# Attention with a gated dense branch on one core: keys packed 128 rows to a projection and spread through DRAM, values two groups at a time, and a higher threshold for giving up units

## The chip, the cores and the metric

The kernel runs on one core of one Trainium2 chip. Its time is the time in microseconds (us) of one execution on the device; the median of several runs is compared. Lower is better. The core has five engines that work side by side, each through its own list of instructions in order: PE (TensorE, matmuls), ACT (ScalarE), DVE (VectorE), POOL (GpSimd) and SP (SyncE, which here only issues DMAs). Engines wait for each other by semaphores.

## What is computed

Two branches work on the same x, and a gate per token mixes them.

```python
# x: 2048 x 640, bf16; 32 heads of 20; dense width 1536
g = sigmoid((x * gate_w).sum(-1, keepdims=True))
qkv = (x @ wqkv).reshape(1, 2048, 3, 32, 20)          # -> q, k, v per head
p = softmax(einsum("bhqd,bhkd->bhqk", q, k) * 20 ** -0.5)
a = einsum("bhqk,bhkd->bhqd", p, v).reshape(1, 2048, 640) @ wo
h = x @ w1 + b1
b = (h * tanh(softplus(h))) @ w2
out = g * a + (1 - g) * b
```

There are 32 × 2048 × 2048 exponentials. They are the largest part of the work.

## The kernel before

**Units, slots and steps.** The 32 heads are eight groups of four. A group's keys and queries lie in KT and QT, each head on its own 32 partitions, of which 20 hold data. A *unit* is the 128 × 512 scores of one head, one block of 128 keys and one block of 512 queries. A *slot* holds three units in three banks of PS. A *step* handles one slot: PE writes its scores (L947), ACT takes one exponential over all three units into ETS (L969), and later PE multiplies by the values, four heads side by side, into one bank (L1072, an attention pass). There are 2048 units, so 683 steps. The first 341 steps take the query blocks 0 and 1 group by group, the others the blocks 2 and 3.

**Units given up by ACT.** In some steps the third unit isn't ACT's: DVE computes its exponential with a chain of six instructions (L986, L1001, three of L1003, L1004). ACT's exponential of that step is then two units wide (128 × 1024 instead of 128 × 1536). `choose` decides it.

**The order is planned when the kernel is built.** A planner (`Plan`, `attention`) goes through the steps in Python, holds an estimate of each engine's time, and writes the list of instructions of each engine. All work other than scores, exponentials and passes is a *task*: a few matmuls into one spare bank of PS and an instruction, mostly of DVE, that empties it. A task has a due step. A forced one is put in at its due step at the latest; before that, tasks go into the gaps of PE. From the tasks' due steps the planner works out how far PE is behind (`behind`), and gives a unit up before the step `slot_of(0, 1, 0)` freely and after it only where, among others, `behind < CATCH_UP` (L1364). Where the planner sees that PE would stream too little, it adds filler matmuls: it repeats scores, or spins on keys (L1315).

**Projections.** A task of `kq_task` (L516) makes the keys or the queries of one group and one block of 512 tokens: POOL first copies the group's 80 weight columns into PADK or PADQ with each head moved to its 32 columns (L500), then five 512-column matmuls (L522) yield 128 rows, of which 80 hold data, and DVE copies them into KT or QT (L533). A task of `v_task` (L592) makes one group's values for 512 tokens with 20 matmuls of 80 columns (L597), and DVE puts them into V_all (L605). Group 0's first block is made at the start (`first_keys`). The tasks for w1, the dense branch and the output projections follow, the last of them in the second half.

**Normalisation.** When a group's passes are done, DVE copies the sums to OUNG (L1150). SP fetches the row of sums into RR (L1153), DVE takes the reciprocal (L1157), SP writes it to SUMS in DRAM (L1158) and reads it back spread over partitions into BCT (L1160), and DVE multiplies (L1118) into OTN or QT. These three DMAs and all loads of weights are in SP's one list, in the planner's order.

Of the kernel before, what the change touches and what calls it, by code (L numbers as in the profile page):

```python
# [9 lines left out]
BF16 = mybir.dt.bfloat16  # L10
# [6 lines left out]
P = 128  # L17
S = 2048
D = 640
# [45 lines left out]
AHEAD = 14  # L65
BEHIND = 7.0
PATIENCE = 10.0
CATCH_UP = 2.0
BUSY = 0.6
CROWD = 1.4  # L70
MARGIN = 0.5
# [7 lines left out]
LAG = 8  # L79
WINDOW = 3.41  # L80
CALM = 4
THIN = 0.09
CUTS = ((0, 256), (256, 256))

# [119 lines left out]
def bass_gated_mix__softmax_full_mha__dense_activation_mish__prompt_kernel(  # L204
# [116 lines left out]
    def attention(pl, fast):  # L321
# [37 lines left out]
        def real(g):  # L359
            return min(g, NG - 1)  # L360
# [14 lines left out]
        def later(step, fn):  # L375
            at.setdefault(step, []).append(fn)
# [50 lines left out]

        k_done, q_done, v_done = {}, {}, {}
        k_more = []
        x_read = {c: [] for c in range(NC)}  # L430
        wkv_read, wq_read = [], []
        xt_load = [None] * NC
# [10 lines left out]
        if fast:  # L443
# [70 lines left out]
            gw_col = pl.add("pool", lambda e: e.tensor_copy(WV[:, :, D], GW[:, :]), [g_load])  # L514

            def kq_task(k, g, c, due, forced=True):  # L516
                b = g % 2
                dst = (QT, KT)[k]
                pads = (PADQ, PADK)[k]

                def mm(f):
                    return lambda e, bank: e.matmul(  # L522
                        PS[:, bank, :], pads[:, b, f, :], xt(c)[:, f, :], start=(f == 0), stop=(f == NFT - 1))
# [12 lines left out]

                return Task([mm(f) for f in range(NFT)], PASS, finish, due,
                            lambda: [*xt_load[c], pad(k, g)], forced)

            turned = []  # L540

# [50 lines left out]
            def v_task(g, c, due):  # L592
# [8 lines left out]
                def finish(bank, last):  # L601
# [12 lines left out]

                return Task([mm(t, f) for t in range(4) for f in range(NFT)], 0.036, finish, due,
                            lambda: [*xt_load[c], w_load["wv0" if g == 0 else "wv"]] + [gw_col] * (n > HD), True)

            def sigmoid(got):
                ex = pl.add("act", lambda e: e.activation(GATE[:, :], GT1[:, :], AF.Exp, scale=-1.0), [got], cost=0.2)
# [438 lines left out]
        def pv(some):  # L1058
# [4 lines left out]
            for r in range(CW // w):  # L1063
                for n, ((_, _, kt, j), src, deps) in enumerate(some):
# [7 lines left out]
                    lasts[n] = pl.add("pe", lambda e, tile=tile, h=real(g) * HG + j, j=j, src=src[:, cols], of_q=of_q, count=count: e.matmul(  # L1072
# [33 lines left out]
        def group_done(c, g, step, last):  # L1106
# [61 lines left out]
        if fast:  # L1168
# [20 lines left out]
            tasks.extend(sq_task(n, 24 + 16 * n) for n in range(8))  # L1189
            tasks.extend(h_task(hc, k, 150 + int(12.5 * (6 * hc + k))) for hc in range(2) for k in range(6))  # L1190
            tasks.sort(key=lambda t: t.due)
            later(60, lambda: (load_w1(0), load_w1(1)))
            rest = []

            def mixed(a, b):
# [137 lines left out]
        for step in range(NSLOT + 40):  # L1333
# [13 lines left out]
            if fast and step == 6:  # L1347
# [207 lines left out]
```

## Time and profile before

| what | us |
|---|---|
| median of 3 runs | 910.29 |
| the runs | 906.25, 912.21, 910.29 |
| the profiled execution | 907.12 |
| its span, first to last instruction | 905.3 |
| ACT busy | 887.6 |
| DVE busy | 813.8 |
| PE busy | 763.3 |
| exponentials (L969) busy, 683 of them | 870.3 |

The profile shows one execution. A group of instructions has a line, an engine, an operation, the tiles that it writes and reads, a count, its busy time and the mean length of one in ns; behind it stands how long the engine was idle just before, and for whom. Lengths of neighbours on one engine can overlap, so the distance between two starts is the better price of one instruction. "Granted clock" is the share of its full clock that PE was given.

### The profile page before, as it was taken

What the parts mean: (1) busy time and instruction counts of PE and PEld (TensorE: products, weight loads), DVE (VectorE), ACT (ScalarE), POOL (GpSimd) and SP (SyncE); (2) the same over time, 40 slices, a digit from 0 to 9 for tenths busy, and PEclk for the clock granted to TensorE, in tenths of its full rate; (3) what the DMA queues carried; (4) which work ended last, traced back from release to release, by engine and by line L of the source; (5) the groups of instructions that cost most, each with busy time, mean ns of one, the idle gap of its engine ahead of it and who ended that gap; (6) DMA issues with size and microseconds to landing.
All of it is one profiled execution on the core that took longest, in us unless ns stands there. A gap on an engine that the chain in (4) does not pass through costs nothing.

```text
span 905.3 us, 15709 instructions
## 1 busy us (share of the span) xinstructions
PE 763.3 (84%) x6516; PEld 263.9 (29%) x6516; DVE 813.8 (90%) x1473; ACT 887.6 (98%) x714; POOL 15.0 (2%) x28
## 2 busy tenths in 40 slices
PE   8878888888888888888888888888888888888886
PEld 3222222232323223222332232232232323333322
DVE  5995859989699999999999999999999999987695
ACT  6999999999999999999999999999999999999996
POOL 2000000000000000000000000000000000000000
PEclk9999999999999999999999999999999999999998
DMA  9002000010101100014111130211121201200001
GB/s 224 4 13 42 13 14 13 6 37 14 42 28 37 35 28 13 13 39 116 47 43 53 46 80 22 57 38 31 51 68 40 71 13 56 57 20 24 13 14 33
DMA packets 63518, 36.44 MB, mean 40 GB/s; under 512 B 19992, under 2 KB 59424, under 8 KB 63392
## 3 DMA queue, kind: packets, MB, share of 16 engines
q1 hardware_dynamic: 61072, 34.88, 14.1%
q8 instruction: 53, 0.87, 0.4%
q10 hardware_dynamic: 2256, 0.47, 0.3%
q0 software_dynamic: 112, 0.01, 0.2%
q14 instruction: 25, 0.20, 0.1%
HBM read 30.25 MB, written 2.89 MB: 37 GB/s over the span
## 4 chain that ended last, share of the span: by engine, by line
ACT 96%; PE 3%; DMA 0%; issue 0%; DVE 0%; SPq 0%; ACTq 0%
ACT ETS L969 93%; ACT REG L761 2%; PE PS L947 1%; PE PS L822 1%; ACT W2R L761 1%; PE PS L1072 1%; DMA OTN<-in_A_x_dram 0%; PE PS L798 0%; PE PS L571 0%; DVE HB L828 0%; PE PS L1315 0%; PE PS L562 0%; PE PS L550 0%; SPq L452 0%; ACT KT L546 0%
## 5 line engine op out<-in xcount | busy, mean ns | idle before, releaser
L969 ACT ACTIVATE ETS<-PS 128x1536 bf16<-128x1536 f32 (+1 forms) x683 | 870.3, 1592 | 3.5 <-PE PS L947 3.3
L947 PE MATMUL PS<-QT,KT 32*128 32x512 bf16 (+1 forms) x2222 | 280.9, 381 | 129.1 <-ACT ETS L969 115.9
L1072 PE MATMUL PS<-ETS,V_all 128*21 128x512 bf16 (+1 forms) x1973 | 210.2, 382 | 0.1
L947 PEld LDWEIGHTS PS<-QT,KT 32*128 32x128 bf16 x2222 | 69.7, 91 | 345.1 <-ACT ETS L969 324.0
L1003 DVE SCALAR_TENSOR_TENSOR EM<-EM 128x512 f32<-128x512 f32 (+1 forms) x201 | 138.3, 688 | 0.4 <-DVE QT L533 0.2
L1003 DVE SCALAR_TENSOR_TENSOR ER<-ER 128x512 f32<-128x512 f32 (+1 forms) x198 | 135.4, 684 | 0.1
L1072 PEld LDWEIGHTS PS<-ETS,V_all 128*21 128x21 bf16 x1973 | 48.9, 89 | 101.9 <-issue 97.4
L798 PE MATMUL PS<-W2R,HB 128*128 128x320 bf16 x384 | 72.1, 305 | 1.0 <-DVE XB L805 0.3
L729 PE MATMUL PS<-XB,REG 128*128 128x256 bf16 x360 | 54.0, 275 | 1.5 <-DVE HB L739 0.9
L522 PE MATMUL PS<-XB,REG 128*128 128x512 bf16 x155 | 47.8, 385 | 0.0
L522 PE MATMUL PS<-XB,WOQ 128*128 128x512 bf16 x155 | 46.6, 384 | 0.0
L781 DVE RECIPROCAL T<-T 128x256 f32<-128x256 f32 x24 | 41.9, 1747 | 0.0
L798 PEld LDWEIGHTS PS<-W2R,HB 128*128 128x128 bf16 x384 | 29.5, 98 | 36.4 <-issue 22.1
L986 DVE TENSOR_SCALAR XE<-PS 128x512 f32<-128x512 f32 x52 | 35.7, 687 | 3.7 <-PE PS L947 3.3
L533 DVE CAST KT<-PS 128x512 bf16<-128x512 f32 x31 | 21.4, 690 | 19.5 <-PE PS L522 19.3
L729 PEld LDWEIGHTS PS<-XB,REG 128*128 128x128 bf16 x360 | 29.2, 97 | 26.0 <-issue 23.0
L597 PE MATMUL PS<-REG,XB 128*128 128x80 bf16 (+1 forms) x640 | 33.7, 201 | 1.8 <-DVE KT L533 0.6
L739 DVE TENSOR_TENSOR HB<-PS,B1F 128x512 bf16<-128x512 f32 x48 | 33.0, 687 | 1.1 <-PE PS L729 0.9
L986 DVE TENSOR_SCALAR REG<-PS 128x512 f32<-128x512 f32 x45 | 30.8, 685 | 0.7 <-PE PS L947 0.7
L597 PEld LDWEIGHTS PS<-REG,XB 128*128 128x128 bf16 x640 | 25.8, 98 | 17.4 <-issue 9.4
L1150 DVE COPY OUNG<-PS 128x512 f32<-128x512 f32 x31 | 21.3, 687 | 9.4 <-PE PS L1072 9.2
L986 DVE TENSOR_SCALAR W2R<-PS 128x512 f32<-128x512 f32 x36 | 24.8, 688 | 3.6 <-PE PS L947 3.5
(115 smaller groups left out, 690.6 us busy)
## 6 DMA issues: line engine op xcount, KB each, us to landing
REG<-in_B_w_dram SPq DMA_DIRECT2D x36, 320.0 KB, 3.2
BCT<-SUMS SPq DMA_DIRECT2D x31, 256.0 KB
W2R<-in_B_w_dram SPq DMA_DIRECT2D x12, 320.0 KB, 3.2
W2R<-in_B_w_dram SPq DMA_DIRECT2D x1, 1920.0 KB, 8.1
out_dram<-OUTT SPq DMA_DIRECT2D x24, 80.0 KB, 1.6
REG<-in_A_wqkv_dram SPq DMA_DIRECT2D x2, 700.0 KB, 8.5
WOQ<-in_A_wo_dram SPq DMA_DIRECT2D x4, 200.0 KB
WOQ<-in_A_wqkv_dram SPq DMA_DIRECT2D x1, 700.0 KB, 8.1
```

Of the source, the lines that this page charges most:

```text
L522: return lambda e, bank: e.matmul(PS[:, bank, :], pads[:, b, f, :], xt(c)[:, f, :], start=(f == 0), stop=(f == NFT - 1))
L597: return lambda e, bank: e.matmul(PS[:, bank, t * n:(t + 1) * n], xt(c)[:, f, t * P:(t + 1) * P], WV[:, f, g * HD:g * HD + n], start=(f == ...
L729: return lambda e, bank: e.matmul(PS[:, bank, i * HW:(i + 1) * HW], w1b(n1)[:, f, i * P:(i + 1) * P], xt(c)[:, f, cols], start=(f == 0), s ...
L739: ev = dve(lambda e: e.tensor_tensor(hb, PS[:, bank, :].rearrange("p (i t) -> p i t", i=2), bias, ALU.add), [last, *b1f, *sq_read.values() ...
L761: ex = pl.add("act", lambda e: e.activation(U, h, AF.Tanh, scale=0.5), [ev, u_free[0]], cost=0.95)
L781: piece(RECIP, lambda e: e.reciprocal(T1[:, :], T1[:, :]))
L798: return lambda e, bank: e.matmul(PS[:, bank, 0:HALF], HB[:, hc % 2, f, t * P:(t + 1) * P], W2[:, f, half * HALF:(half + 1) * HALF], start ...
L947: op = pl.add("pe", lambda e, i=i, g=real(g), tile=tile, j=j, cols=cols, c=c, of_q=of_q: e.matmul(scores(s)[:, i, cols], KT[32 * j:32 * j ...
L969: e_op[s] = pl.add("act", lambda e: e.activation(ETS[:, s % NETS, 0:n, :], scores(s)[:, 0:n, :], AF.Exp, scale=SCALE), [s_op[s], pv_slot.g ...
L986: ev_op[s] = dve(lambda e: e.tensor_scalar(y, scores(s)[:, 2, :], SCALE * ULPS, BIAS, ALU.mult, ALU.add), [s_op[s], ei_free[b], *(wkv_read ...
L1003: piece(WIDE, lambda e, v=m if i else f, i=i: e.scalar_tensor_tensor(m, v, STEPS[i], v, ALU.add, ALU.mult))
L1072: lasts[n] = pl.add("pe", lambda e, tile=tile, h=real(g) * HG + j, j=j, src=src[:, cols], of_q=of_q, count=count: e.matmul(PS[32 * j:32 * ...
```

## The change

Keys of the groups 1 to 7 are no longer padded before the projection. `k_task` projects 128 plain rows at once (weight columns 80 to 591 in four tasks per token block), and `k_end_task` the last 48 rows for two token blocks side by side. DVE copies the result to one of four stages in OTN (rows that the groups 6 and 7 will use later), SP writes the stage to KS in DRAM (`shelve`), and three steps after the last piece of a group's keys was written SP reads them back into KT (`fetch`), 32 rows for each head at a stride of 20. The 12 rows that a head has too many are those of the next head; they meet rows of QT that are zero. The tasks are due ten steps before their keys are needed (`PACKED`), where `kq_task` had three. Values of the groups 2 to 7 are projected for two groups at once, three tiles of 128 tokens in a task (`v_pair_task`). `CATCH_UP` goes from 2 to 3. `SQ`, `SQ_STEP`, `H_AT` and `H_STEP` name numbers that are the same as before.

```diff
-CATCH_UP = 2.0
+CATCH_UP = 3.0
...
+PACKED = 10
...
+    KS = nc.dram_tensor("KS", [NC, D + DH, CW], BF16, kind="Internal")
...
             def kq_task(k, g, c, due, forced=True):
-                b = g % 2
+                b = 0 if k else g % 2
...
-                    if c == NC - 1 and g + 2 < NG:
+                    if not k and c == NC - 1 and g + 2 < NG:
                         pad(k, g + 2)
...
+            stages = [OTN[:, a, b, :] for b in (6, 7) for a in range(2)]
+            stage_free, k_written, k_reads = {}, {}, {}
+            k_need = {1: (0,), 2: (0, 1), 3: (1,), 4: (1, 2), 5: (2, 3), 6: (3,), 7: (3, "end")}
+            count = [0]
+            none = ZEROS.ap()[:, 0:CW]
+            k_blank = [pl.add("sp", lambda e, c=c: e.dma_start(
+                KS.ap()[c, D:D + 12, :], none.to_broadcast([12, CW])), [zeros], "kz", cost=0.5) for c in range(NC)]
+
+            def shelve(name, c, rows, src, ev, n, i=0):
+
+                k_written[(name, c)] = pl.add(
+                    "sp", lambda e: e.dma_start(KS.ap()[c, rows, :], src), [ev], f"kw{n}{i}", cost=0.5)
+                k_moved.append(k_written[(name, c)])
+                stage_free.setdefault(n, []).append(k_moved[-1])
+                for g, names in k_need.items():
+                    if (g, c) not in k_done and name in names and all((m, c) in k_written for m in names):
+                        k_done[(g, c)] = None
+                        later(now["step"] + 3, lambda g=g, c=c, names=names: fetch(g, c, names))
+
+            def fetch(g, c, names):
+
+                at = KS.ap()[c, g * HD:(g + 1) * HD, :].rearrange("(j r) t -> j r t", r=DH)
+                at = bass.AP(tensor=at.tensor, offset=at.offset, ap=[list(at.ap[0]), [at.ap[1][0], 32], list(at.ap[2])])
+                slot = f"kr{c}{g % 2}"
+                k_done[(g, c)] = k_reads[slot] = pl.add(
+                    "sp", lambda e: e.dma_start(KT[:, g, c * CW:(c + 1) * CW], at),
+                    [*(k_written[(m, c)] for m in names), *k_blank, k_reads.get(slot)], slot, cost=0.5)
+
+            def k_task(i, c, due):
+
+                base = HD + P * i
+
+                def mm(f):
+                    return lambda e, bank: e.matmul(
+                        PS[:, bank, :], WK[:, f, base:base + P], xt(c)[:, f, :], start=(f == 0), stop=(f == NFT - 1))
+
+                def finish(bank, last):
+                    x_read[c].append(last)
+                    wkv_read.append(last)
+                    n = count[0] % 4
+                    count[0] += 1
+                    ev = dve(lambda e: e.tensor_copy(stages[n], PS[:, bank, :]), [last, *stage_free.pop(n, ())], WIDE)
+                    shelve(i, c, slice(base, base + P), stages[n], ev, n)
+                    return ev
+
+                return Task([mm(f) for f in range(NFT)], PASS, finish, due, lambda: [*xt_load[c], w_load["wk"]], True)
+
+            def k_end_task(c, due):
+
+                base, m = HD + 4 * P, D - HD - 4 * P
+
+                def mm(f, i):
+                    return lambda e, bank: e.matmul(
+                        PS[64 * i:64 * i + m, bank, :], WK[:, f, base:D], xt(c + i)[:, f, :],
+                        start=(f == 0), stop=(f == NFT - 1), tile_position=(0, 64 * i))
...
-                    v_done[(g, c)] = ev
+                    v_done.update({(g, c * 4 + t): ev for t in range(4)})
...
+            def v_pair_task(g, tiles, due):
+
+                n = 2 * HD + (g == NG - 2)
+                cs = sorted({t // 4 for t in tiles})
+
+                def mm(i, t, f):
+                    return lambda e, bank: e.matmul(
+                        PS[:, bank, i * n:(i + 1) * n], xt(t // 4)[:, f, t % 4 * P:(t % 4 + 1) * P],
+                        WV[:, f, g * HD:g * HD + n], start=(f == 0), stop=(f == NFT - 1))
...
-                        deps = [*deps, v_done[(real(g), tile // 4)]]
+                        deps = [*deps, v_done[(real(g), tile)]]
...
-                    return [low_last[0]] if c >= 2 else [zeros, *turned]
+                    return [low_last[0]] if c >= 2 else [zeros, *turned, *(k_moved if g >= 6 else ())]
...
-                        tasks.append(kq_task(1, g, c, due - 3))
-                        tasks.append(v_task(g, c, due - 1))
-                        last_kv = tasks[-1]
+                        if g == 0:
+                            tasks.append(kq_task(1, g, c, due - 3))
+                        if g < 2:
+                            tasks.append(v_task(g, c, due - 1))
...
+            for i, g in enumerate((1, 2, 4, 5)):
+                tasks.extend(k_task(i, c, slot_of(0, g, 4 * c) - PACKED) for c in range(NC))
+            tasks.extend(k_end_task(c, slot_of(0, NG - 2, 4 * c) - PACKED) for c in (0, 2))
+            for g in range(2, NG, 2):
+                for t in range(0, NKT, 3):
+                    tasks.append(v_pair_task(g, list(range(t, min(t + 3, NKT))), slot_of(0, g, t) - 1))
+            last_kv = tasks[-1]
```

More of the change, by code (lines that the diff above doesn't have):

```diff
@@ L81 @@
 CALM = 4
+PACKED = 10
+SQ = 24
+SQ_STEP = 16
+H_AT = 150
+H_STEP = 12.5
 THIN = 0.09
@@ L429, in attention @@
         k_more = []
+        k_moved = []
         x_read = {c: [] for c in range(NC)}
@@ L516, in kq_task @@
             def kq_task(k, g, c, due, forced=True):
-                b = g % 2
+                b = 0 if k else g % 2
                 dst = (QT, KT)[k]
@@ new lines, in k_end_task, with finish @@
+            def k_end_task(c, due):
[4 more added lines that the diff above has]
+                        start=(f == 0), stop=(f == NFT - 1), tile_position=(0, 64 * i))
+                def finish(bank, last):
+                    wkv_read.append(last)
+                    n = count[0] % 4
+                    count[0] += 1
+                    for i in range(2):
+                        x_read[c + i].append(last)
+                    ev = dve(lambda e: e.tensor_copy(stages[n], PS[:, bank, :]), [last, *stage_free.pop(n, ())], WIDE)
+                    for i in range(2):
+                        shelve("end", c + i, slice(base, D), stages[n][64 * i:64 * i + m, :], ev, n, i)
+                    return ev
+                return Task([mm(f, i) for f in range(NFT) for i in range(2)], PASS / 2, finish, due,
+                            lambda: [*xt_load[c], *xt_load[c + 1], w_load["wk"]], True)
@@ L616, in v_task, with finish @@
                             lambda: [*xt_load[c], w_load["wv0" if g == 0 else "wv"]] + [gw_col] * (n > HD), True)
+            def v_pair_task(g, tiles, due):
[5 more added lines that the diff above has]
+                        WV[:, f, g * HD:g * HD + n], start=(f == 0), stop=(f == NFT - 1))
+                def finish(bank, last):
+                    for c in cs:
+                        x_read[c].append(last)
+                    wkv_read.append(last)
+                    m = len(tiles)
+                    got = PS[:, bank, 0:m * n].rearrange("p (t k) -> p t k", k=n)
+                    ev = dve(lambda e: e.tensor_copy(
+                        V_all[:, tiles[0]:tiles[0] + m, g * HG:(g + 2) * HG, 1:EW],
+                        got[:, :, 0:2 * HD].rearrange("p t (h d) -> p t h d", d=DH)), [last, m_one], WIDE * m / 3)
+                    v_done.update({(g + i, t): ev for t in tiles for i in range(2)})
+                    if n > 2 * HD:
+                        ev = dve(lambda e: e.tensor_copy(GT1[:, tiles[0]:tiles[0] + m], got[:, :, 2 * HD]), [last])
+                        if tiles[-1] == NKT - 1:
+                            later(now["step"] + 2, lambda: sigmoid(ev))
+                    return ev
+                return Task([mm(i, t, f) for i, t in enumerate(tiles) for f in range(NFT)], 2 * HD * COL, finish, due,
+                            lambda: [*(d for c in cs for d in xt_load[c]), w_load["wv"]] + [gw_col] * (n > 2 * HD), True)
             def sigmoid(got):
@@ L1346, in attention @@
                 load_w2()
-            if fast and step == 6:
+            if fast and step == SQ - 18:
                 squares(0)
```

7 lines of the change are left out of this document (4 added, 3 removed).

## The prediction

> **What bounds the kernel now.** I read the page's shares and its chain first, then the groups of instructions by form, then the timeline for spacings, then the stages.
>
> ```profile
> span 905.3 us, 15709 instructions
> PE 763.3 (84%) x6516; PEld 263.9 (29%) x6516; DVE 813.8 (90%) x1473; ACT 887.6 (98%) x714; POOL 15.0 (2%) x28
> ACT 96%; PE 3%; DMA 0%; issue 0%; DVE 0%; SPq 0%; ACTq 0%
> ```
>
> ACT is busy 98% of the span and carries 96% of the chain that ended last; almost all of that is L969, the exponentials. DVE at 90% is the second resource: it computes the units that ACT gives up. So a change is worth what it takes from ACT or puts in ACT's way. The price of an exponential is read from spacings, not from its busy time, since neighbours overlap. Timeline of ACT, where the built program has only full exponentials (start, length):
>
> ```profile
> 809.56 1.59 ACT L761 ACTIVATE REG<-HB 128x1024 f32<-128x1024 bf16 x1
> 810.50 14.08 ACT L969 ACTIVATE ETS<-PS 128x1536 bf16<-128x1536 f32 x10
> 823.81 1.71 ACT L761 ACTIVATE REG<-HB 128x1024 f32<-128x1024 bf16 x1
> ```
>
> Ten full ones take 823.81 − 810.50 = 13.31 us, **1.331 us** each. Now the first 141 exponentials: the chain's piece, and the groups by form in that window.
>
> ```profile
> 9.91 176.57 ACT ETS L969 x141
> ```
>
> ```profile
> L969 ACT ACTIVATE ETS<-PS 128x1536 bf16<-128x1536 f32 x113 | 156.4, 1608 | 0.5 <-PE PS L947 0.5
> L969 ACT ACTIVATE ETS<-PS 128x1024 bf16<-128x1024 f32 x28 | 31.1, 1211 | 0.0
> ```
>
> 113 × 1.331 = 150.4; the other 26.2 us over 28 short ones (two units, the third given to DVE) is **0.934 us** each, what they wait behind scores included; their median spacing in the trace is 0.905. A unit given up is worth 1.331 − 0.934 = 0.40 us, at most 0.43. Stages (busy us of PE, weight loads, DVE, ACT, POOL; then granted clock):
>
> ```profile
> 100.00:150.00 50.00, 42.33 (x373) 13.02 (x369) 36.32 (x68) 50.00 (x41) 1.03 (x2) 1.00 0.04 12
> 450.00:500.00 50.00, 42.65 (x346) 15.09 (x345) 49.69 (x90) 50.00 (x42) 0.00 (x0) 1.00 0.19 52
> 550.00:600.00 50.00, 41.77 (x325) 14.45 (x322) 46.90 (x85) 48.21 (x40) 0.00 (x0) 0.93 0.17 48
> ```
>
> Three things are to be seen. While keys and values are projected (to about 410 us), DVE has room (36 of 50 us). Later it is full (49.7 of 50), and ACT still loses nothing: a full DVE alone does not stop ACT. ACT loses 1.8 us in the third window, where the clock is 0.93. PE's timeline there:
>
> ```profile
> 551.78 0.39 PE L947 MATMUL PS<-QT,KT 32*128 32x512 bf16 x3 [0.38 <-ACT ETS L969]
> 552.70 0.39 PE L947 MATMUL PS<-QT,KT 32*128 32x512 bf16 x3 [0.53 <-ACT ETS L969]
> 553.02 0.40 PE L1072 MATMUL PS<-ETS,V_all 128*21 128x512 bf16 x4
> 553.35 1.15 PE L798 MATMUL PS<-W2R,HB 128*128 128x320 bf16 x4
> 554.43 1.03 PE L947 MATMUL PS<-QT,KT 32*128 32x512 bf16 x3
> ```
>
> Three scores take 0.39 us at first and 1.03 us at 554.43: from 553.5 the granted clock is one half for 3.4 us. It is halved at 413.6, 553.5, 584.2, 652.5 and 888.0, and not once between 4 and 410. Exponentials around the first four start 0.3, 1.7, 1.1 and 0.7 us late, about 1.0 us each: such stretches are the main loss of ACT between start and tail.
>
> **The change, part by part.** Counts are from the instruction order of the two built programs (first plan only).
>
> *Units given up (CATCH_UP).* The program has 140 short exponentials in place of 134, of 683: 5 of the 6 more in the first 341 steps. 6 × 0.40 = **−2.4 us** of ACT; −2.6 by the median spacing, 0 if each were lost behind a late score. DVE pays about 0.69 (L986) + 0.42 (L1001) + 3 × 0.69 (L1003) + 0.69 (L1004) = 3.9 us a unit, 23 us.
>
> *Keys, DVE.* Evictions fall from 31 (L533, KT) to 3 plus 18 into OTN: −10 × 0.69 = −6.9 us. Values: 32 of 0.49 = 15.6 become 8 of 0.49, 15 of 480 columns (about 0.66, between the 320- and 512-column rows) and 3 short ones (0.32): 14.7. DVE's total is +23 − 6.9 − 0.9, some +15 us; its phase to 380 us has 324 of 380 us busy, and 12 of the 15 fall there. That idle time hides it; were the cover gone, a late DVE would hold the bank that the next score writes.
>
> *Keys and values, PE.* From the timeline:
>
> ```profile
> 101.71 0.39 PE L522 MATMUL PS<-XB,WOQ 128*128 128x512 bf16 x1
> 102.49 1.04 PE L522 MATMUL PS<-XB,WOQ 128*128 128x512 bf16 x4
> 105.08 0.72 PE L597 MATMUL PS<-REG,XB 128*128 128x80 bf16 x15
> ```
>
> A 512-column matmul adds (1.04 − 0.39)/3 = 0.217 us, an 80-column one about 0.037, so a 160-column one about 0.070 on the line between. Keys: 155 × 0.217 = 33.6 become 95 × 0.217 plus 20 that stand in pairs side by side (0.108 each, an estimate) = 22.8. Values: 640 × 0.037 = 23.7 become 22.7. PE loses 12 us of work; the planner's fillers rise (spins 27 to 52, repeated scores 110 to 124), some 6 us back. PE is not the bound, so I cost this at nothing, but for the clock: in steps 239 to 241 (about 311 us) the new order has only three scores and one attention pass a step, 3 × 0.43 of 3.6 us, 0.36 of PE. The 3.4 us ahead of 553.5 had three scores three times, two passes and two or three matmuls of L798: 3 × 0.22 + 2 × 0.22 + 0.3, 0.4 of PE. I charge one more half-clock stretch at 1.0 us with a chance of 0.7: **+0.7 us** (bounds 0 and 1.7).
>
> The Trainium skill ("TensorE: Matmul & The Clock Gate", "Why this matters for your kernels") says that a clock drop needs a pause of some 3 us between bursts of matmuls. By that the thin spot costs nothing and the sum is −2.4. The trace differs: no pause ahead of 553.5 was longer than 0.6 us, and the clock fell.
>
> *Keys through DRAM.* SP gains 4 fills, 20 writes and 28 reads. Rows for their kind:
>
> ```profile
> REG<-in_B_w_dram SPq DMA_DIRECT2D x36, 320.0 KB, 3.2
> BCT<-SUMS SPq DMA_DIRECT2D x31, 256.0 KB
> out_dram<-OUTT SPq DMA_DIRECT2D x24, 80.0 KB, 1.6
> ```
>
> 128 KB each way lies between 1.6 and 3.2 us to landing; I take 2. The far bound is BCT<-SUMS, like the reads a fetch from DRAM over 128 partitions: issued at 44.1, its user (L1118) ran at 51.5, so 7.4 us at most. The write is issued in the step of its eviction, the read three steps later, and the first score on it comes 5 steps later at the nearest (third and fourth block of group 1: issued in steps 46 and 51, used in 51 and 56), else 7 or more. Five steps with a short one are 4 × 1.331 + 0.934 = 6.3 us: against 2 us nothing waits, against 7.4 us two scores wait 1.1 each. So 0, bounds 0 and +2.2. PE works in order, so a score that waits would hold the passes and projections behind it, and then ACT. On SP the reads stand between the three DMAs of a group's normalisation; 0.53 us of issue each is hidden by SP's wait for the reciprocal (47 us in 20 waits). If BCT came later, L1118 would hold DVE: it waited on BCT once, 0.8 us. Some 12 groups × 0.5 us = 6 us of DVE at worst, inside its idle 56 us.
>
> *The rest.* POOL loses seven copies of 0.58 us that nothing waits for. The first 36 steps are the same in both programs, and the end is as before: 0.
>
> **Sum.** −2.4 + 0.7 = −1.7 us. The profiled execution took 907.12 (span 905.3 and 1.8 around it): 905.4. The median shown is 910.29, 3.2 above it, with runs from 906.25 to 912.21; from the median it is 908.6. I forecast the middle, **907 us**.
>
> **Rivals.**
> - *More half-clock stretches (ends slower).* Place: the projection phase, some 115 stretches of 3.4 us, none halved now; price 1.0 us each. Against: the fillers grew. Slower by over 1% needs 9.1 + 2.4 = 11.5 us, a dozen of them: about 919 or more. It decides where PE falls to about 0.4 of a stretch over and over. 0.08.
> - *Keys land late.* Reads of 10 us instead of 2 would hold five or six blocks by 1 to 4 us, some 12 us: about 919. For it: two DMAs in series with DRAM between them. Against: every DMA of up to 320 KB in the table lands in about 3 us. 0.03, of which half is over 1%.
> - *The clock's luck turns.* Without the four stretches between 400 and 700 us, 907.1 − 2.6 − 3.8 = 900.7, just over 1% under the median. 0.07.
> - *The units given up bring nothing*, since scores after a short exponential are late: 907 to 910, inside 1%. 0.12.
>
> **How the numbers follow.** Forecast 0.70. Range: 900.7 is the low end, taken as 901; high is the slowest run shown 912.2 − 2.4 + 1.7 + 2.2 = 913.7, taken as 914. One per cent is about what a measurement of this kernel can tell from no change. Faster by over 1%: 0.07; slower: 0.08 + 0.015, taken as 0.09; within: the rest, 0.84.
>
> **What would show it.** After: 140 short exponentials of 683; DVE about 829 us busy; no wait of a score on KT<-KS over 0.5 us; spacing of full exponentials still 1.331; clock 1.00 to 300 us, one halved stretch near 315. Wrong if PE waits on KT<-KS, if the clock is under 1.00 in several windows before 300, or if ACT's idle before 380 grows by more than 2 us.

## The result and the profile after

| | before | after |
|---|---|---|
| median, 20 runs each side by side | 908.56 | **905.67** |
| lowest and highest | 904.87, 912.63 | 903.07, 909.55 |
| profiled execution, its span | 907.12, 905.3 | 903.7, 901.8 |
| short exponentials, of 683 | 134 | 140 |
| DVE busy | 813.8 | 826.5 |
| PE busy | 763.3 | 755.0 |

The ratio is 0.9966, with a 95% interval of 0.995 to 0.9981. The kernel is a little faster, 2.9 us by the medians, and that lies inside the 1% that was called no change.

From the page of the profile after, the span, the busy time of the engines and the chain that ended last:

```profile
span 901.8 us, 15322 instructions
PE 755.0 (84%) x6275; PEld 259.3 (29%) x6275; DVE 826.5 (92%) x1495; ACT 884.8 (98%) x714; POOL 11.9 (1%) x21
ACT 96%; PE 2%; DMA 1%; DVE 1%; issue 0%; SPq 0%; ACTq 0%
```

ACT still bounds the kernel, with 96% of the chain as before. DVE took over about 13 us. The exponentials (now L1075) by form, from the groups of ACT:

```profile
L1075 ACT ACTIVATE ETS<-PS 128x1536 bf16<-128x1536 f32 x543 | 778.9, 1711 | 2.2 <-PE PS L1053 2.2
L1075 ACT ACTIVATE ETS<-PS 128x1024 bf16<-128x1024 f32 x140 | 174.9, 1279 | 0.0
```

Six more of them are short. Their spacing is as before: 1.331 us for a full one, and for a short one 0.904 is the commonest (the median is 0.913, before 0.905). The stages of before again, and one more (start:end, busy us of PE, weight loads, DVE, ACT, POOL; then the granted clock, the share of the DMA engines, GB/s):

```profile
100.00:150.00 50.00, 41.35 (x353) 14.22 (x355) 29.86 (x57) 50.00 (x40) 0.52 (x1) 1.00 0.12 39
300.00:350.00 50.00, 42.02 (x361) 15.64 (x362) 47.27 (x88) 49.02 (x41) 0.97 (x1) 0.97 0.15 44
450.00:500.00 50.00, 41.20 (x330) 13.71 (x328) 49.05 (x87) 50.00 (x42) 0.00 (x0) 1.00 0.14 42
550.00:600.00 50.00, 42.03 (x356) 15.17 (x353) 49.71 (x89) 50.00 (x41) 0.00 (x0) 1.00 0.18 50
```

The third window of the prediction (550 to 600) has lost its half-clock stretch, and ACT its 1.8 us there. A new one stands in 300 to 350: 0.97, and ACT idle for 0.98 us. PE's timeline around it (start, length, line, tiles, count, idle time before and its releaser):

```profile
317.03 0.39 PE L1053 MATMUL PS<-QT,KT 32*128 32x512 bf16 x3 [0.63 <-ACT ETS L1075]
317.35 0.40 PE L1178 MATMUL PS<-W2R,V_all 128*21 128x512 bf16 x2
318.27 0.39 PE L1053 MATMUL PS<-QT,KT 32*128 32x512 bf16 x3 [0.53 <-DVE XE L1092]
318.60 0.40 PE L1178 MATMUL PS<-ETS,V_all 128*21 128x512 bf16 x4
319.29 0.39 PE L1053 MATMUL PS<-QT,KT 32*128 32x512 bf16 x3 [0.29 <-ACT ETS L1075]
319.61 0.51 PE L1178 MATMUL PS<-ETS,V_all 128*21 128x512 bf16 x3
320.05 1.05 PE L599 MATMUL PS<-XB,REG 128*48 128x512 bf16 x4
321.03 0.61 PE L1053 MATMUL PS<-QT,KT 32*128 32x512 bf16 x3
```

The clock is halved from 319.75 on: three scores take 0.61 us instead of 0.39. The longest pause of PE in the four microseconds ahead is 0.63 us. In these steps PE has only scores (L1053) and passes (L1178) to do; this is the thin spot that the prediction named.

The time of the two profiled executions in parts, from the starts of the exponentials on ACT (number of each form times its spacing, and how much later than that the next one started):

| us | before | after |
|---|---|---|
| start, to the first exponential | 9.91 | 10.12 |
| all exponentials (1.331 full, 0.904 short) and the pieces of tanh (0.946) | 874.56 | 872.00 |
| late, around half-clock stretches | 5.34 | 2.68 |
| late elsewhere | 7.06 | 7.94 |
| tail, after the last of them | 8.43 | 9.07 |
| span | 905.3 | 901.8 |

Units give 2.6 us, fewer stretches 2.7 in this pair of executions, and 1.7 go back at the start, in the tail and in late scores. The number of stretches is chance in good part, so the runs must decide about it (below).

**The keys' way through DRAM.** SP's timeline, where three transfers of a normalisation (L1259, L1264, L1266) stand between the key writes (L558) and reads (L572):

```profile
66.12 0.33 SPq L558 DMA_DIRECT2D KS<-OTN  x1
67.05 0.56 SPq L1259 DMA_DIRECT2D RR<-OUNG  x1
67.84 0.51 SPq L572 DMA_DIRECT2D KT<-KS  x1
69.72 0.32 SPq L1264 DMA_DIRECT2D SUMS<-RR  x1
71.95 0.53 SPq L1266 DMA_DIRECT2D BCT<-SUMS  x1
72.74 0.33 SPq L558 DMA_DIRECT2D KS<-OTN  x1
77.64 0.52 SPq L572 DMA_DIRECT2D KT<-KS  x1
78.20 2.33 SPq L791 DMA_DIRECT2D W2R<-in_B_w_dram  x2
```

The second key read is issued 4.9 us after its write, because SP waits for the write to land. Then PE's timeline shows the first score on that block:

```profile
82.30 0.39 PE L1053 MATMUL PS<-QT,KT 32*128 32x512 bf16 x3 [0.64 <-DMA KT<-KS]
```

It waited 0.64 us for the keys, the only such wait in the execution, and the next exponential started 0.14 us late. Why the write took so long is seen in the DMA view of the stretch 72 to 78 us (busy tenths of all 16 engines in 40 slices of 0.15 us, and the issues with KB and us to landing):

```profile
DMA  0000000090398312122222222221222110000000
BCT<-SUMS SPq DMA_DIRECT2D x1, 256.0 KB
KS<-OTN SPq DMA_DIRECT2D x1, 128.0 KB, 4.9
KT<-KS SPq DMA_DIRECT2D x1, 128.0 KB
```

The digits 3983, from 73.5 to 74.1 us, are the write with all engines at work, and the long row of 2s and 1s behind them is a quarter of the engines or less. The packets of the trace say which: BCT<-SUMS goes as 128 packets of 2 KB from 73.26 to 76.88 us, 3.7 in flight on average. Of the 128 packets of the write, 96 are through by 74.07, and the other 32, a quarter, only between 76.18 and 77.23. The write issued at 66.12, with no other transfer under way, was through in 0.5 us with 12 packets in flight and landed in 1.7. A key read also goes 3 to 3.8 packets at a time: the one issued at 67.84 was through at 71.39, after 3.6 us.

From the waits of SP, those of key reads for their writes (line, releaser, us in total, times, longest):

```profile
SPq L572 <- DMA KS<-OTN: 30.7, 12, 4.6
```

Twelve of the 28 reads waited, 2.6 us on average, and SP's list stood still meanwhile.

### The profile page after: what moved, and what is told of

Read it like the earlier page. It is cut to its first block, busy times and chain, and to the rows that moved or that the text cites. A ratio compares the mean times of both kernels' runs of the same rounds, so it can differ in the third digit from the quotient of the medians.

```text
span 901.8 us, 15322 instructions
## 1 busy us (share of the span) xinstructions
PE 755.0 (84%) x6275; PEld 259.3 (29%) x6275; DVE 826.5 (92%) x1495; ACT 884.8 (98%) x714; POOL 11.9 (1%) x21
## 4 chain that ended last, share of the span: by engine, by line
ACT 96%; PE 2%; DMA 1%; DVE 1%; issue 0%; SPq 0%; ACTq 0%
ACT ETS L1075 93%; ACT REG L867 2%; DMA REG<-in_B_w_dram 1%; ACT W2R L867 1%; DMA OTN<-in_A_x_dram 1%; PE PS L1053 0%; PE PS L904 0%; PE PS L599 0%; PE PS L1178 0%; DVE T L887 0%; PE PS L648 0%; DVE HB L934 0%; PE PS L1430 0%; PE PS L639 0%; PE PS L928 0%
## 5 line engine op out<-in xcount | busy, mean ns | idle before, releaser
L1075 ACT ACTIVATE ETS<-PS 128x1536 bf16<-128x1536 f32 (+1 forms) x683 | 867.7, 1622 | 2.2 <-PE PS L1053 2.2
L1053 PE MATMUL PS<-QT,KT 32*128 32x512 bf16 (+1 forms) x2236 | 280.7, 378 | 134.0 <-ACT ETS L1075 117.7
L1178 PE MATMUL PS<-ETS,V_all 128*21 128x512 bf16 (+1 forms) x1967 | 208.6, 380 | 0.6 <-ACT ETS L1075 0.5
L1053 PEld LDWEIGHTS PS<-QT,KT 32*128 32x128 bf16 x2236 | 69.5, 91 | 353.7 <-ACT ETS L1075 335.2
L1109 DVE SCALAR_TENSOR_TENSOR EM<-EM 128x512 f32<-128x512 f32 (+1 forms) x210 | 143.3, 682 | 0.2
L1109 DVE SCALAR_TENSOR_TENSOR ER<-ER 128x512 f32<-128x512 f32 (+1 forms) x207 | 141.5, 684 | 0.3 <-DVE HB L845 0.2
L1178 PEld LDWEIGHTS PS<-ETS,V_all 128*21 128x21 bf16 x1967 | 49.1, 89 | 103.4 <-issue 98.3
L1092 DVE TENSOR_SCALAR XE<-PS 128x512 f32<-128x512 f32 x55 | 37.7, 685 | 5.0 <-PE PS L1053 4.7
L1092 DVE TENSOR_SCALAR REG<-PS 128x512 f32<-128x512 f32 x51 | 34.9, 684 | 2.7 <-PE PS L1053 1.7
L1092 DVE TENSOR_SCALAR W2R<-PS 128x512 f32<-128x512 f32 x33 | 22.6, 686 | 6.1 <-PE PS L1053 5.9
L867 ACT ACTIVATE REG<-HB 128x1024 f32<-128x1024 bf16 x18 | 24.2, 1345 | 0.0
L928 PE MATMUL PS<-WOQ,QT 128*128 128x320 bf16 x128 | 24.0, 302 | 0.3 <-DVE HB L934 0.3
L928 PE MATMUL PS<-WOQ,OTN 128*128 128x320 bf16 x128 | 23.8, 302 | 0.3 <-DVE HB L845 0.3
L701 PE MATMUL PS<-REG,XB 128*128 128x160 bf16 (+1 forms) x240 | 23.1, 234 | 1.0 <-DVE HB L845 0.5
```

What stands on the lines that cost most here:

```text
L867: ex = pl.add("act", lambda e: e.activation(U, h, AF.Tanh, scale=0.5), [ev, u_free[0]], cost=0.95)
L928: return lambda e, bank: e.matmul(PS[:, bank, 0:HALF], otn(c, g, fast)[:, t * P:(t + 1) * P], WOG[:, g, half * HALF:(half + 1) * HALF], st ...
L1053: op = pl.add("pe", lambda e, i=i, g=real(g), tile=tile, j=j, cols=cols, c=c, of_q=of_q: e.matmul(scores(s)[:, i, cols], KT[32 * j:32 * j ...
L1075: e_op[s] = pl.add("act", lambda e: e.activation(ETS[:, s % NETS, 0:n, :], scores(s)[:, 0:n, :], AF.Exp, scale=SCALE), [s_op[s], pv_slot.g ...
L1092: ev_op[s] = dve(lambda e: e.tensor_scalar(y, scores(s)[:, 2, :], SCALE * ULPS, BIAS, ALU.mult, ALU.add), [s_op[s], ei_free[b], *(wkv_read ...
L1109: piece(WIDE, lambda e, v=m if i else f, i=i: e.scalar_tensor_tensor(m, v, STEPS[i], v, ALU.add, ALU.mult))
```

## The experiments

Theory A is that of the prediction: the time goes by the units given up, the clock stretches come and go by chance of the order, and the keys' transfers are hidden. The rivals: the rewriting of keys and values gains by itself (a lighter PE or DVE); the clock decides; the keys' transfers cost something that the gain covers.

Two measures are used for all kernels. *Units* are those that `choose` gives up, one fewer than the short exponentials in the program; before has 133, after 139. *Half-clock stretches* of a run are worked out from its mean granted clock: (1 − clock) × 2 × span / 3.413 us, the length of one in the records. They vary for one and the same program: from 0.5 to 12.3 in 35 runs of the kernel before (mean 5.9), from 2.6 to 10.1 in 20 runs of the one after (mean 5.3). Over all kernels, run by run against the mean of its kernel, one stretch costs 0.72 us of span (correlation 0.86; one run of experiment 9, with a mean clock of 0.847 at an ordinary time, is left out). So mean spans can be compared at an equal number; three is taken: before 903.8, after 901.9, each known to about 0.2 us. The 35 runs of before are those beside the experiments 1, 2, 3 and 6; in the two other sets of runs of before the figure is 903.6 and 903.8. Ratios are to the kernel before, run beside each kernel on the same chip.

**1. The threshold alone, on the kernel before.**

```diff
-CATCH_UP = 2.0
+CATCH_UP = 3.0
```

> The kernel before with CATCH_UP = 3 and nothing else. The planner then gives up 127 units in place of 133. Theory A (the gain is the number of units that DVE takes from ACT, 0.40 us each): 6 units fewer, +2.4 us, ratio to before 1.0026. Theory B (the higher threshold as such lets DVE help more, and keys and values only follow): faster than before, about 0.997. Theory C (the gain is the lighter load of PE and DVE from packed keys and paired values): no change, 1.000.

908.26 us, ratio 1.0011 (0.9998 to 1.0024), a little under the 1.0026 of theory A; 127 units, 3.0 stretches a run; 906.1 at three stretches. The higher threshold alone gives fewer units than before, not more, and the kernel is 2.3 us slower at equal stretches, 0.38 us for each of the six units. It hardly shows in the median because this program had three stretches fewer than before.

**2. All of the change but the threshold.**

```diff
-CATCH_UP = 3.0
+CATCH_UP = 2.0
```

> The changed kernel with CATCH_UP = 2 as before: packed keys and paired values stay. 131 units. Theory A: 2 units fewer than before, +0.8 us, 1.001; the rewriting of keys and values alone brings nothing. Theory B: about 1.000. Theory C: the gain of the change stays, 0.9966.

910.05 us, ratio 1.0018 (0.9998 to 1.0039); 131 units; 905.7 at three stretches. One of its twelve runs took 1444 us and is left out. The rewriting alone gains nothing either.

**3. All of the change, but never more units than before.**

```diff
-            if (len(order) < SLOT or ei_free[home()] == "busy"
+            if len(off) >= 133 or (len(order) < SLOT or ei_free[home()] == "busy"
```

> The changed kernel with at most 133 units given up, as many as before; the last six (all behind step 640) are ACT's again. Theory A: as before, 1.000 (between 0.999 and 1.001). Theory C: 0.9966 as the change. If half-clock stretches differ between the two, each is worth 0.8 us (the slope of the times of the changed kernel's runs over their granted clock).

906.86 us, ratio 1.0000 (0.9985 to 1.0016); 903.9 at three stretches, where before has 903.8. With the units held at 133, the lighter PE, the fewer evictions and the longer way of the keys sum to nothing that can be seen (0.3 us either way). The short exponentials of the two programs are the same but for six behind step 651, and the kernel after is 2.0 us faster at equal stretches: 0.33 us a unit. The six units carry the whole gain.

**4. Keys rewritten, values as before (the higher threshold in).**

```diff
-            for g in range(2, NG, 2):
-                for t in range(0, NKT, 3):
-                    tasks.append(v_pair_task(g, list(range(t, min(t + 3, NKT))), slot_of(0, g, t) - 1))
+            for g in range(2, NG):
+                for c in range(NC):
+                    tasks.append(v_task(g, c, slot_of(0, g, 4 * c) - 1))
```

> The changed kernel, CATCH_UP = 3 and keys packed through DRAM, but values one group at a time as before. 137 units. By 0.40 us a unit: 4 x 0.40 = 1.6 us under before, 0.9982. If paired values gave the gain by their own (fewer matmuls and evictions): 1.000.

906.06 us, ratio 0.9989 (0.9975 to 1.0002); 137 units; 902.5 at three stretches.

**5. Values rewritten, keys as before (the higher threshold in).**

```diff
-                        if g == 0:
-                            tasks.append(kq_task(1, g, c, due - 3))
+                        tasks.append(kq_task(1, g, c, due - 3))
...
-            for i, g in enumerate((1, 2, 4, 5)):
-                tasks.extend(k_task(i, c, slot_of(0, g, 4 * c) - PACKED) for c in range(NC))
-            tasks.extend(k_end_task(c, slot_of(0, NG - 2, 4 * c) - PACKED) for c in (0, 2))
...
```

The lines left out put back the padding of the key weights as it was before.

> The changed kernel, CATCH_UP = 3 and values two groups at a time, but keys padded as before and no transfer through DRAM. 124 units. By 0.40 us a unit: 9 x 0.40 = 3.6 us over before, 1.004. If keys through DRAM cost time of their own that units only cover: faster than the change, under 0.9966.

910.86 us, ratio 1.0044 (1.0028 to 1.0059), 7 runs; 124 units; 907.4 at three stretches. The seven kernels so far, ordered by units, at three stretches:

| units | 124 | 127 | 131 | 133 | 133 | 137 | 139 |
|---|---|---|---|---|---|---|---|
| kernel | 5 | 1 | 2 | before | 3 | 4 | after |
| span, us | 907.4 | 906.1 | 905.7 | 903.8 | 903.9 | 902.5 | 901.9 |

They lie along one line of 0.37 us per unit, though much else differs; the farthest, experiment 2, is 0.9 us above it. This is near the price of 0.40 of the prediction. For the rewriting it says that it acts through how many units the planner can place; experiment 3, where the number alone was changed, shows the same. The rewriting pays more by its keys (124 units without them) than by its values (137).

**6. Still more units.**

```diff
-CATCH_UP = 3.0
+CATCH_UP = 9.0
```

> The changed kernel with CATCH_UP = 9: 145 units, 12 more than before and 6 more than the change. Theory A: 12 x 0.40 = 4.8 us under before, 0.9947, that is 2.4 us under the change. Rival: DVE is full by now (92% busy) and late scores eat the six units, as the change or slower, 0.9966 to 0.998.

905.49 us, ratio 0.998 (0.9965 to 0.9994); 145 units; 903.2 at three stretches. The line breaks off here: six more units should have given 899.7. The rival's 0.9966 to 0.998 is what came. What went against it is in the trace. PE's timeline, where the same block of keys as above is late:

```profile
80.50 0.39 PE L529 MATMUL PS<-XB,WOQ 128*128 128x512 bf16 x1
82.38 0.61 PE L1053 MATMUL PS<-QT,KT 32*128 32x512 bf16 x6 [1.49 <-DMA KT<-KS]
82.92 1.04 PE L529 MATMUL PS<-XB,WOQ 128*128 128x512 bf16 x2
```

With more short exponentials the steps go faster, so this score is due at 80.9 us, where after had it at 81.7, and the read is not much earlier (issued at 77.24, after 77.64). The wait grows to 1.49 us, and a half-clock stretch starts at once (82.9). The other place, from the timeline of all engines (`...` stands for lines left out):

```profile
126.38 0.67 DVE L768 TENSOR_REDUCE MXS<-PS 1x1 f32<-1x512 f32 x1
...
127.11 1.25 PE L580 MATMUL PS<-XB,REG 128*128 128x512 bf16 x5 [1.04 <-DVE MXS L768]
...
128.30 0.39 PE L1053 MATMUL PS<-QT,KT 32*128 32x512 bf16 x3
...
128.73 1.45 ACT L1075 ACTIVATE ETS<-PS 128x1536 bf16<-128x1536 f32 x1 [1.11 <-PE PS L1053]
```

A key projection (L580) waits 1.04 us for the bank that a late instruction of DVE empties; the next scores stand behind it in PE's list, and ACT is idle for 1.11 us. This exponential, at 128.7, starts 1.5 us late, and the next late one, at 131.1, 1.0 us.

**7. The same, with the loads of w1 twenty steps later.** After the key read of 78 us SP issues two loads of 320 KB (L791). Here they come later; the order on PE, DVE, ACT and POOL is that of experiment 6.

```diff
-            later(H_AT - 90, lambda: (load_w1(0), load_w1(1)))
+            later(H_AT - 70, lambda: (load_w1(0), load_w1(1)))
```

> The kernel with 145 units (CATCH_UP = 9) again, and the first two loads of w1 issued at step 80 in place of 60, behind the key transfers of group 1. The order of all engines but SP is the same as in e4_more_units. Theory A (keys land late there because a key write stands behind BCT<-SUMS in the queue, 5.1 us to landing, and the key read shares the DMA engines with 2 x 320 KB of w1): the wait of 1.5 us on KT<-KS at 82 us shrinks to under 0.5 us, the half-clock stretch at 83 us goes, and the time falls by 1 to 2 us against e4_more_units, ratio to before 0.996 to 0.997. Rival (the read is slow by itself): the wait stays over 1 us, and the ratio at 0.998.

903.75 us, ratio 0.9962 (0.9945 to 0.9979); 902.1 at three stretches, 1.1 less than experiment 6. PE's waits for keys in experiment 6 (us in total, times, longest):

```profile
PE PS L1053 <- DMA KT<-KS: 2.1, 2, 1.5
```

The same line of the waits with the later loads:

```profile
PE PS L1053 <- DMA KT<-KS: 0.9, 1, 0.9
```

The longest wait falls from 1.5 to 0.9 us, between the two forecasts, and the half-clock stretch at 83 us is gone. From the issue of the read to the score it is 4.1 us (77.73 to 81.87) instead of 5.1 (77.24 to 82.38). Nothing but the place of two loads differs, so they had slowed the key read. The two late exponentials stay as they were (now at 126.9 and 129.3), so these have another cause.

**8. More filler matmuls.** `STREAM` is the share of time that the planner wants PE to stream. It leaves the units at 139 and raises the repeated scores from 124 to 184.

```diff
-STREAM = 0.47
+STREAM = 0.50
```

> The changed kernel with the planner's fill-up limit STREAM at 0.50 in place of 0.47: 139 units as in the change, 184 repeated scores in place of 124, 56 spins in place of 52. If half-clock stretches come from stretches of 3.4 us in which PE streams too little: from 5.3 stretches a run to about half, 2.5 x 0.7 = 1.8 us under the change, ratio to before 0.9945 to 0.996. If they come only from pauses of about 3 us: no change in their number, 0.9966. If the fillers stand in the way of scores: slower than the change, 0.998 or more.

904.26 us, ratio 0.9969 (0.9955 to 0.9983); 4.6 stretches a run, where after has 5.3, and 901.2 at three stretches, where after has 901.9. About half the stretches should have gone. The difference is within what the stretches of one program vary by, so it settles little: more fillers may help a bit or not.

**9 and 10. What helped, together.** The later loads, the threshold of 9, keys due one step earlier, and fillers at 0.50 (9) or 0.49 (10).

```diff
-STREAM = 0.47
+STREAM = 0.49
...
-CATCH_UP = 3.0
+CATCH_UP = 9.0
...
-PACKED = 10
+PACKED = 11
...
-            later(H_AT - 90, lambda: (load_w1(0), load_w1(1)))
+            later(H_AT - 70, lambda: (load_w1(0), load_w1(1)))
```

> Three edits on the change: w1 at step 80, CATCH_UP = 9 with keys due 11 steps ahead (146 units), STREAM = 0.50 (202 repeated scores, 55 spins). By units alone 13 x 0.40 = 5.2 us under before; if late scores take back 2 to 4 us as in e4_more_units and the fillers save 1 us of half-clock stretches: 2 to 4 us under, 0.9955 to 0.998. If the new order of the keys also avoids the stalls of 2.6 us at 124 to 127 us: about 0.993.

> As e9_all_three with STREAM = 0.49: 144 units, 143 repeated scores, 61 spins. By units 11 x 0.40 = 4.4 us under before, 0.995; fewer fillers than e9, so 0.5 to 1 us more in half-clock stretches. Beside e9 it tells what 59 more repeated scores are worth where the rest is nearly alike: e9 faster by 1 to 2 us if fillers pay, the same or slower if they stand in the way.

With 0.50: 904.42 us, ratio 0.9952 (0.9928 to 0.9975), 146 units, 202 repeated scores. With 0.49: **901.72 us**, ratio 0.9926 (0.9899 to 0.9954), 144 units, 143 repeated scores. The one with fewer fillers has fewer stretches, 1.9 a run against 3.0, where more were expected, and the lower median; the two intervals overlap. From the page of the second one:

```profile
span 899.1 us, 15419 instructions
PE 755.7 (84%) x6303; PEld 259.8 (29%) x6303; DVE 842.8 (94%) x1525; ACT 882.5 (98%) x714; POOL 11.5 (1%) x21
```

No score waits for keys in it, and its late scores away from half-clock stretches sum to 8.0 us, as in the kernel after (7.9), with five units more. It is 6.8 us under the median of the kernel before, which was 908.56 beside it and beside the kernel after alike; it didn't run beside the kernel after. At three stretches it is 900.5, 1.3 under after. Which of its edits does how much isn't told apart. By the two prices, 11 units × 0.37 = 4.1 us are units and 4.8 stretches fewer than the kernel before beside it × 0.72 = 3.5 are clock, 7.6 together, where the mean spans differ by 6.75.

**11. No unit given up just ahead of the late exponentials at 127 us**, to see whether units there fill DVE and hold the bank (on experiment 7).

```diff
-            if (len(order) < SLOT or ei_free[home()] == "busy"
+            if 84 <= s < 92 or (len(order) < SLOT or ei_free[home()] == "busy"
```

> The kernel of e5_w1_later with no unit given up in the slots 84 to 91; 144 units in place of 145. Theory (in e4 and e5 the units packed there put DVE behind, DVE empties the spare bank late, the projection that waits for the bank holds the scores behind it in PE's list): the late exponentials of 1.5 and 1.0 us at 124 to 127 us go, and the time falls by 2 us against e5_w1_later, 0.994. Rival (the lateness belongs to the projections and reductions there, not to the units): they stay, 0.9965.

905.45 us, ratio 0.997 (0.9953 to 0.9988); 144 units. The two late exponentials shrink from 2.6 to 1.7 us together but stay, so DVE's chains in these eight steps are a part of the cause at most. Its runs had 6.7 stretches where those of experiment 7 had 3.0, which hides the rest in the median; at three stretches it is 900.8, 1.3 us under experiment 7.

**12. The keys' transfers, doubled.** Ahead of every key read SP copies the same rows from KS to a spare tensor in DRAM. The copy is not quite a second read: it moves 32 KB a packet, but on four engines as well.

```diff
+    KD = nc.dram_tensor("KD", [NC * NG, P, CW], BF16, kind="Internal")
...
+                outs.append(pl.add("sp", lambda e: e.dma_start(KD.ap()[c * NG + g].rearrange("(j r) t -> j r t", r=32), at),
+                       [*(k_written[(m, c)] for m in names), *k_blank], f"kd{c}{g}", cost=0.0))
```

> The change with every key read issued twice: just ahead of each read of KS into KT the same rows are also copied to a spare tensor in DRAM (28 more DMAs of 128 KB, 3.6 MB). The order on PE, DVE and ACT is the same as in the change. Theory (the way through DRAM is hidden apart from one or two tight blocks of group 1): the wait on KT<-KS grows from 0.6 to 1 to 3 us, the time by 0 to 2 us, 0.9966 to 0.999. Rival (DMA traffic as such costs, by holding the normalisation's DMAs and with them DVE): more than 3 us, over 1.000.

920.48 us, ratio 1.0125 (1.0097 to 1.0154), some 15 us more than the kernel after. That these transfers are hidden, and stay so when doubled, is refuted. The timeline of its profiled execution shows the worst place:

```profile
294.25 3.50 SPq L1262 DMA_DIRECT2D RR<-OUNG  x1
...
300.00 0.39 PE L1056 MATMUL PS<-QT,KT 32*128 32x512 bf16 x3 [0.41 <-ACT ETS L1078]
...
303.44 0.25 DVE L1266 RECIPROCAL RR<-RR 128x16 f32<-128x16 f32 x1 [6.96 <-DMA RR<-OUNG]
...
306.36 0.68 DVE L848 TENSOR_TENSOR HB<-PS,B1F 128x512 bf16<-128x512 f32 x1
...
307.10 1.89 PE L530 MATMUL PS<-XB,WOQ 128*128 128x512 bf16 x4 [6.71 <-DVE HB L848]
...
308.92 0.61 PE L1056 MATMUL PS<-QT,KT 32*128 32x512 bf16 x3
...
309.57 1.45 ACT L1078 ACTIVATE ETS<-PS 128x1536 bf16<-128x1536 f32 x1 [7.37 <-PE PS L1056]
```

The row of sums, a small transfer, stands behind key copies and reads and a load of w1: issued at 294.25, its packets run only from 302.48 to 302.94, and its user starts 9.2 us after the issue. DVE waits 6.96 us for it, as the reciprocal stands in its list ahead of the eviction (HB, L848) that frees a bank; PE waits 6.71 us for this bank, with the scores behind it; the next exponential is 7.8 us late. Waits of scores for keys, from PE's waits, are the smaller part:

```profile
PE PS L1056 <- DMA KT<-KS: 5.3, 2, 3.6
```

One of these made an exponential 3.2 us late. With 10.6 stretches a run instead of 5.3, 3.8 us, these sum to 14.8. The agreement with the 14.8 of the medians is closer than it has a right to be, since the profiled execution was itself 5 us over its median and some of its stretches follow from these very stalls.

## Why the prediction was right, and where it was not

**The sum.** Forecast 907, measured 905.67; −1.7 us on the profiled execution's own time, −3.4 measured there, −2.9 by the medians. The forecast took the middle between two starting points, 907.12 and 910.29, so it started from 908.7; twenty runs gave 908.56. No row spoke for the middle, so that this part fits is luck. The clock of each run is on record for after and for the 35 runs of before beside the experiments, not for the 20 runs of before beside after. Between these the mean span fell by 2.40 us (give or take 0.5), from 905.91 to 903.51. By the slope of 0.72, the 0.63 stretches fewer are −0.45, and −1.95 is left. The means of the 20 runs beside each other differ by 3.1 us (give or take 0.7), so the clock's part may be up to −1.2.

**Units: right.** 140 short exponentials, a spacing that stayed at 1.331, and −1.95 at equal stretches against −2.4 for six units, inside the bounds of −2.6 and 0. Experiment 3 shows it as cause: nothing gained at 133 units with all the rest in, and 2.0 us for the six. Experiments 1, 2, 4 and 5 agree, at 0.37 us a unit. The prediction didn't see that threshold and rewriting give fewer units each alone (127 and 131), and that only both give more. The rival that the units bring nothing fell for these six. The next six gave nothing in experiment 6, where late scores ate them; in experiment 10, with keys and loads moved, five more came with 1.3 us at equal stretches.

**DVE: right.** 826.5 us busy against about 829. The cover held: up to 380 us it was busy for 328 of 370 us.

**PE and the clock: place right, sum wrong.** At the named thin spot the clock did halve, at 319.75 where "near 315" was said, and that cost 1.4 us there. In experiment 3, which has the same order there, it halved at the same place (319.33). That the thin work is the reason fits both executions, but no run filled this spot alone. The Trainium skill's rule ("TensorE: Matmul & The Clock Gate", "Why this matters for your kernels"), read as the only cause, as the prediction weighed it, would have had no drop at that place, as no pause of PE is over 0.63 us; the trace shows one without a long pause again. But the step "I charge one more half-clock stretch at 1.0 us with a chance of 0.7: +0.7 us" was mis-sized: it counted the spot that the new order makes, and not that a new order moves all the others too. The four stretches between 400 and 700 us of the execution before became one (695.2). Over the runs the term is −0.45 (at most −1.2) instead of +0.7. Those 1.15 us, less the 0.45 by which the units (with all that isn't clock) brought less than forecast, are the 0.7 between the sum of −1.7 and the −2.40 of the mean spans. The price of a stretch was 0.72 us by the slope over all runs; the two of the execution after cost 1.3 us each, so the 1.0 that was charged lies between.

**Keys through DRAM: the wait nearly right, the landing wrong.** "128 KB each way lies between 1.6 and 3.2 us to landing; I take 2" held for a write alone (1.7) and for nothing else: 4.9 for one behind BCT<-SUMS, about 3.6 to 3.8 for a read. The two in series took 8.7 us, from the write's issue at 72.74 to the read's last packet at 81.41, where 2 us each were taken. Of the five steps (6.3 us) between read and score, 4.0 were left, as SP held the read back until the write had landed. The named case, two waits of 1.1 us at the far bound, came out as one of 0.64 us, so the term (0, bounds 0 and 2.2) survived, but two of the prediction's own signs went against it: "no wait of a score on KT<-KS over 0.5 us" and "Wrong if PE waits on KT<-KS". It survived by luck of the place, as experiment 6 shows: six units more, and the score on the same block waits 1.5 us and a stretch follows.

By the Trainium skill ("DMA: Bandwidth & Descriptors", "Why a DMA increments its semaphore by 16 and not by 1"), a transfer runs on the largest number of engines up to 16 that divides the slowest dimension of both sides. The key reads' slowest dimension is the four heads, which gives four engines; the trace agrees, with 3 to 3.8 packets in flight, and 12 for the write of 128 rows.

**Normalisation behind the key transfers: cover overrated.** "Some 12 groups × 0.5 = 6 us of DVE at worst, inside its idle 56 us" held for the kernel after, where ACT was idle for 1.1 us in all before 380 us. But the reason was wrong. What a late reciprocal costs isn't DVE's own time: DVE works in order, so it holds an eviction, this holds PE, and PE holds the scores. Experiment 12 put 7.8 us on ACT from a single late row of sums.

**The rivals.** Slower by many half-clock stretches: not here; experiment 12 comes closest (10.6 a run). Late keys: not here either; but "every DMA of up to 320 KB in the table lands in about 3 us" didn't hold for the full table of before, which has 5.9 us for two loads of 100 KB at the start. The clock's luck shows in the spread: the 20 runs of after go from 903.07 to 909.55, in step with their stretches (correlation 0.92).

## What to carry to other kernels

Where one engine bounds the kernel and another takes work from it, count the pieces that change hands in the built program and price them by spacing: here that one number, 0.37 us times units, puts seven kernels that differed in much else within 0.9 us of one line. Before a detour through DRAM is called hidden, look at which other transfers of that list run at the same time and on how few engines, and at what stands in order behind the instruction that waits for them. When a change is worth less than the clock's own spread, compare runs at an equal granted clock, or the luck of the order is taken for the effect.

## What the runs showed of the hardware

- A 128 KB read whose pattern has four heads as its slowest dimension kept 3 to 3.8 packets in flight and took 3.6 us, a 128 KB write of 128 rows 12 packets and 1.7 us to landing. A read cut so that it spreads further wasn't tried.
- A write over all engines issued 0.8 us after a 256 KB transfer that runs on a quarter of them had three quarters of its packets through in 0.5 us and the last quarter 3.2 us later: 4.9 us instead of 1.7. That fits a write that is done only when the busiest of its engines has got to its share.
- The clock was halved for 3.4 us at 319.75 without any pause of PE over 0.63 us ahead of it. How many times it happens changes from run to run of one program (0.5 to 12.3 by the mean clock), and each time costs 0.72 us of span here. More fillers didn't reliably prevent it (experiments 8 to 10). In each kept trace the stretches start a whole number of 3.413 us apart (before: 41, 50 and 70 times that behind the one at 413.6; after: 110 times), and where they fall differs from execution to execution. A thin spot could so be hit in one run and missed in the next; that wasn't tested, and what decides a single case stays open.
